# Attention products in two column ranges, maxima transposed later, scratch rows of 4 KB, normalizers loaded in another order

## The chip, the cores and the metric

The kernel runs on one core of a Trainium2 chip. A core has a matrix engine (TensorE, PE in the profile; its weight loads are shown apart as PEld), a vector engine (VectorE, DVE), an engine for functions of single elements (ScalarE, ACT), a general engine (GpSimd, POOL) and an engine that issues transfers (SyncE, SP). Each runs its own instructions in order, and they wait for one another through semaphores. SBUF is the memory that the engines work in, 128 partitions wide; TensorE writes its results to PSUM, which has eight banks of 512 float32 numbers in each partition; DRAM is reached only by DMA. The metric is the time of one execution on the device, in microseconds (us).

## The reference

One transformer block over 2048 tokens of width 640. `ln` is a layer norm without gain or bias.

```
h  = x + attention(ln(x) @ wqkv) @ wo       # 32 heads of 20; a query sees itself and the 255 keys before it
z  = gelu(ln(h) @ w_in)                     # 2048 x 1728, halves z1 and z2
g  = w_sp @ ln(z2) + b_sp                   # mixes tokens: 2048 x 2048 times 2048 x 864
h2 = h + (z1 * g) @ w_out
```

Attention is softmax(q k / sqrt(20)) v in float32, with scores outside the window set to -1e9.

## The kernel before, in words

**Stages.** To about 250 us, x is normalized, and q, k and v are computed. v stays in SBUF (`v_sb`, with a column of ones beside each head's 20 columns, so that a product with it gives the sum of the softmax's weights too). q and k are each split into three bf16 parts whose sum is the float32 number, and go to a DRAM scratch `qk_d` [2, 3, 40, 16, 1024 floats]: half of the heads, part, row of q or k, head, and 2048 bf16 tokens in 1024 floats. From about 250 to 500 us comes attention, then the projection with wo and the second layer norm, to about 570 us. The rest is the gated MLP with its large token-mixing product.

**Attention.** The 32 heads are eight groups of four. `load_stack` (L253) brings a group's q and k parts from `qk_d` into one of three slots, in twelve transfers of 20 rows, each of four heads times 4 KB; the slots hold the six pairings of parts under each other as 120 rows, so that one bf16 product gives a float32-like score. The main loop (L554) has 130 steps. Step s does, for each head `hh` of four: a product for the row maxima, 20 steps ahead (`max_item`, u1 = s + 20); the scores of 128 keys against up to 384 queries and their exponential (`score_item`, u = s); and, after the second step, for all four heads at once, the product of the exponentials with v (`pv_item`, u = s - 2). A group has 16 such steps, one for each block of 128 keys.

- `max_item` writes a bank of tag `s1`, of which there are three; VectorE adds the mask and takes the maximum to one column of `mcol` (L286). From the third block of a group on, the product is made in four strips of 32 queries and 288 keys.
- `max_rows` (L289) turns a finished group's 64 columns of maxima on TensorE (L291), splits them into three bf16 parts with four operations on VectorE, writes them to DRAM (`m_d`, L299) and reads them back as rows 120 to 122 of the slot (L301). With them the score product subtracts the maximum itself. It is called in the step in which the next group's maxima begin, four steps before its group's scores start.
- `score_item` writes one of three banks `s2` and ScalarE makes the exponential (L339); when all four heads are done, GpSimd sets to zero what lies outside the window (L341, L344). From step 109 on, two heads go together into larger tiles.
- `pv_item` adds a block's 384 query columns into banks of 512 columns (two of them, tag `pv`); where the 384 cross from one bank to the next, they are done in two ranges. After each fourth block a bank is finished, is copied by ScalarE or VectorE (`ot`, L370, L372) and goes to DRAM (`o_d`).

**The end of attention.** The sums of the softmax's weights lie in row 20 of each head in `o_d`. Once the last group has finished a bank, `inverse_sums` reads the sums of these 512 tokens for all heads, takes the reciprocal (L314) and writes it to `r_d`. `proj_early` loads and splits wo (L170 to L181), loads the outputs of 256 tokens at a time (`load_o`, L134) and their reciprocals repeated over 20 rows (its returned function, L140), multiplies (`norm_o`, L146) and splits (`split_o`, L152 to L155). Both are generators that the main loop advances by one `yield` a step.

**Order.** TensorE, VectorE and ScalarE run the attention stage in the order in which the program writes it; SP and GpSimd are ordered by a planner, as are all engines behind the stage (from L593).

Of the kernel before, what the change touches and what calls it, by code (L numbers as in the profile page):

```python
# [7 lines left out]
F32 = mybir.dt.float32  # L8
# [8 lines left out]
S = 2048  # L17
D = 640
H = 32
DH = 20  # L20
NT = S // P
# [13 lines left out]
def block_kernel(ctx, tc, x, wqk, wv, wo, w_in, wsp, bsp, w_out, out):  # L35
# [5 lines left out]
    def pool(stack, name, **kw):  # L41
        return stack.enter_context(tc.tile_pool(name=name, bufs=1, reuse_waits="tile", **kw))

    const = pool(ctx, "const")
    dram = pool(ctx, "dram", space=DRAM)

    qk_d = dram.tile([2, 3, 2 * DH, H // 2, S // 2], F32, name="qk_d")
    m_d = dram.tile([8, 3, 64, 64], F32, name="m_d")
    o_d = dram.tile([H, 32, S], F32, name="o_d")
    r_d = dram.tile([H, S], F32, name="r_d")  # L50
# [63 lines left out]
    def t1(lo, *shape):  # L114
        return view(mem["t1"], lo, *shape)

    def m1(lo, *shape):
        return view(mem["m1"], lo, *shape)
# [6 lines left out]
    def load_x2(i):  # L125
        hs[i] = mem["xh"][i % 5]
        nc.sync.dma_start(hs[i], x[i * P:(i + 1) * P, :])

    def load_o(j):

        t = slice(2 * j * P, (2 * j + 2) * P)
        ot, rs = m1(j % 2 * 2 * D, KD, 2 * P), m1(6 * D + j % 2 * 2 * P, 2 * P)
        for k in range(KD):
            nc.sync.dma_start(ot[:, k], o_d[:, 4 * k:4 * k + 4, t])  # L134
        for i in range(2):
            ots[2 * j + i] = (ot[:, :, i * P:(i + 1) * P], rs[:, i * P:(i + 1) * P])

        def load_rs():
            base = r_d[:, t]
            nc.sync.dma_start(rs, bass.AP(tensor=base.tensor, offset=base.offset, ap=[[S, H], [0, 4], [1, 2 * P]]))  # L140

        return load_rs

    def norm_o(i, eng):
        ot, rs = ots[i]
        eng.tensor_tensor(out=ot, in0=ot, in1=rs[:, None, :].to_broadcast([P, KD, P]), op=OP.mult)  # L146

    def split_o(i, eng):
        ot, _ = ots[i]
        osp = mem["osp2"] if i % 3 == 2 else t1((2 * KD + i % 3 * 2) * D, 2, KD, P)  # L150
        if eng is nc.vector:
            eng.tensor_copy(out=osp[:, 0], in_=ot)  # L152
        else:
            nc.scalar.activation(osp[:, 0], ot, AF.Copy)
        eng.tensor_tensor(out=osp[:, 1], in0=ot, in1=osp[:, 0].bitcast(F32), op=OP.subtract)  # L155
        ots[i] = osp
# [8 lines left out]
    def proj_early():  # L165
        wo_s = t1(0, 2, KD, D)
        for k in range(KD):
            if k < 4:
                raws_c[f"wo{k}"] = m1(k * D, D)
                nc.sync.dma_start(raws_c[f"wo{k}"], wo[k * P:(k + 1) * P, :])  # L170
            else:
                raws_c[f"wo{k}"] = mem["wraw"].rearrange("p a b c -> p (a b c)")[:, :D]
                nc.sync.dma_start(raws_c[f"wo{k}"], wo[k * P:(k + 1) * P, :])
        for i in range(2):
            load_x2(i)
        for _ in range(5):
            yield
        for k in range(KD):
            raw = raws_c.pop(f"wo{k}")
            nc.vector.tensor_copy(wo_s[:, 0, k], raw)  # L180
            nc.vector.tensor_tensor(out=wo_s[:, 1, k], in0=raw, in1=wo_s[:, 0, k].bitcast(F32), op=OP.subtract)  # L181
            if k in (1, 3):
                yield
        yield
        rs = [load_o(j) for j in range(2)]
        yield
        yield
        for f in rs:
            f()
        yield  # L190
        yield
        for i in range(2):
            norm_o(i, nc.vector)
            split_o(i, nc.vector)
            yield


    with ExitStack() as ab:
# [34 lines left out]
        NU = 128  # L233
# [19 lines left out]
        def load_stack(g):  # L253


            st = slot_w[g % 3]
            if g < 3:
                nc.gpsimd.memset(st[96:P, 1], ONES)
            for j, parts in enumerate(((0, 0), (0, 1), (0, 2), (1, 0), (1, 1), (2, 0))):
                for a in range(2):  # L260
                    src = qk_d[g // 4, parts[a], a * DH:(a + 1) * DH, g % 4 * 4:g % 4 * 4 + 4]
                    nc.sync.dma_start(st[j:6 * DH:6, a], src)
                    yield

# [38 lines left out]
        p_tiles, pv_tiles, inverse = {}, {}, []  # L303
# [43 lines left out]
        def pv_item(u):  # L347
            g, kb = divmod(u, NT)
            pt = p_tiles.pop(u)
            a, e = kb * P, min(S, kb * P + 384)  # L350
            while a < e:
                c = a // 512
                b = min(e, (c + 1) * 512)
                first = kb == max(0, 4 * c - 2)
                if first:
                    pv_tiles[g, c] = pv_tile(f"pv{g}_{c}")
                ps = pv_tiles[g, c]
                for hh in range(4):
                    v0 = 21 * (4 * g + hh)
                    nc.tensor.matmul(ps[32 * hh:32 * hh + 32, a - 512 * c:b - 512 * c],  # L360
                                     v_sb[:, kb, v0:v0 + 32], pt[:, hh, a - kb * P:b - kb * P],
                                     start=first, stop=(kb == 4 * c + 3), skip_group_check=True,
                                     tile_position=(0, 32 * hh))
                a = b
            if kb % 4 == 3:
                c = kb // 4
                ps = pv_tiles.pop((g, c))
                ot = tmp3.tile([P, 512], F32, tag="ot", bufs=4, name=f"ot{g}_{c}")
                if u < NU - LEAD or u >= NU - 5:
                    nc.scalar.activation(ot, ps, AF.Copy)  # L370
                else:
                    nc.vector.tensor_copy(out=ot, in_=ps)  # L372
                nc.sync.dma_start(o_d[4 * g:4 * g + 4, :, c * 512:(c + 1) * 512].rearrange("h d t -> (h d) t"), ot)
                if g == 7:
                    inverse.append(inverse_sums(c))


        if True:
# [70 lines left out]
            def split_qk(m, c, ps):  # L449
                sg = tmp.tile([P, 3, 512], BF16, tag="ta", bufs=3, name=f"sg{m}_{c}")  # L450
                rest = tmp.tile([P, 512], F32, tag="tb", bufs=2, name=f"rest{m}_{c}")
                nc.scalar.activation(sg[:, 0, :], ps, AF.Copy)  # L452
                yield
                nc.vector.tensor_tensor(out=rest, in0=ps, in1=sg[:, 0, :], op=OP.subtract)  # L454
                yield
                nc.scalar.activation(sg[:, 1, :], rest, AF.Copy)  # L456
                nc.gpsimd.tensor_tensor(out=sg[:, 2, :], in0=rest, in1=sg[:, 1, :], op=OP.subtract)  # L457
                T = S // 2
                base = qk_d[m // 5, 0, m % 5 * 8, 0, c * 256:(c + 1) * 256]
                nc.sync.dma_start(bass.AP(tensor=base.tensor, offset=base.offset,  # L460
                                          ap=[[T, P], [2 * DH * H // 2 * T, 3], [1, 256]]), sg.bitcast(F32))

# [14 lines left out]
            c = halves[0]  # L477
# [76 lines left out]
        for s in range(NU + 2):  # L554
            if s % NT == 0 and s // NT + 2 < 8:
                ld = load_stack(s // NT + 2)
            for _ in range(1 + s % 2):
                next(ld, None)
            for f in inverse:
                next(f, None)  # L560
            u1 = s + LEAD
            for hh in range(4):
                if u1 < NU:
                    max_item(u1 // NT, u1 % NT, hh)
                if s <= NU - LEAD:
                    score_item(s, hh, 1)
                elif s < NU and hh % 2 == 0:
                    score_item(s, hh, 2)
                if hh == 1 and u1 % NT == 0 and u1 <= NU:
                    max_rows(u1 // NT - 1)  # L570
                if hh == 2 + s - NU and s >= NU:
                    pre_ps.append(proj_o(s - NU, ps6[0].tile([P, 2, 512], F32, tag="sp", bufs=3,
                                                             name=f"wo_ps{s - NU}")))
                if hh == 2 and s >= 2:
                    pv_item(s - 2)
            if u1 == NU:
                psB.close()
                ps6[0] = pool(psB, "ps6t", space=PSUM)
            if s == NU - NT:
                low0.close()  # L580
                lowx.close()
                open_early(pool(early_stack, "early"))
                early = proj_early()
            if early is not None and s > NU - NT:
                next(early, None)
        for _ in early:
            pass
        for f in inverse:
# [563 lines left out]
```

## Time and profile before

| | |
|---|---|
| median of 3 runs | 1176.09 us (1174.71 to 1176.49) |
| the profiled execution | 1176.24 us, of which its span 1174.2 us |
| mean granted TensorE clock | 0.984 |
| TensorE busy | 1116.0 us, 95% |
| VectorE, ScalarE, GpSimd busy | 744.1, 543.1 and 388.8 us |
| DMA | 165.15 MB in 72122 packets, 141 GB/s in the mean |

A line of the profile names the source line (L360), the engine, the operation, what it writes and reads (out<-in), its shape and count. Behind a bar stand the busy time, the mean duration of one and the idle time of the engine just before, with what ended it. In the timeline, the first two numbers are start and duration in microseconds, and idle time before an instruction stands in square brackets with its releaser; "issue" is idle time for which the profile shows no wait. Matmuls are pipelined, so their durations overlap; the distance of their starts is what one costs. A float32 matmul appears as two, and four matmuls of 32 columns of the array, one a head, run side by side.

### The profile page before, as it was taken

To read this page: it belongs to the slowest core of one execution; us is meant where nothing else is said; L and a number is where in the kernel's file an instruction comes from. 1 tells how busy PE (TensorE), PEld (TensorE's weight loads), DVE (VectorE), ACT (ScalarE), POOL (GpSimd) and SP (SyncE) were. 2 spreads that over 40 slices of the span, in tenths; PEclk is the share of its full clock that TensorE was granted. 3 is DMA by queue.
4 is the path that set the end of the run, shared out by engine and by line. 5 is a ranking of instruction groups with operands and counts; after the bars stand their busy time and mean duration, and the time that the engine had idled before them with its cause. 6 is when DMAs were issued, how large, how long until landed. Compare 5 with 4: busy or idle time off the path is not lost. (4 is left out here: it accounts for less than half of the span.)

```text
span 1174.2 us, 25759 instructions
## 1 busy us (share of the span) xinstructions
PE 1116.0 (95%) x9888; PEld 961.9 (82%) x9888; DVE 744.1 (63%) x1949; ACT 543.1 (46%) x1125; POOL 388.8 (33%) x477
## 2 busy tenths in 40 slices
PE   6999999989999998798999999899999899999998
PEld 6998887556566565488999998899999799999998
DVE  5531125878788786479958669745548984655443
ACT  4333343248888888724346644433334431222110
POOL 4124444346555566737522046000116420000000
PEclk9999999989999999989899999999999999999999
DMA  6212453643444441659735531233341454444322
GB/s 205 66 44 87 166 194 126 260 148 111 153 161 165 154 172 52 225 174 295 261 147 191 168 103 38 66 118 116 133 139 63 130 177 150 140 132 142 90 82 81
DMA packets 72122, 165.15 MB, mean 141 GB/s; under 512 B 9128, under 2 KB 33448, under 8 KB 70056
## 3 DMA queue, kind: packets, MB, share of 16 engines
q1 hardware_dynamic: 69696, 158.27, 40.2%
q10 hardware_dynamic: 2304, 5.24, 1.1%
q8 instruction: 77, 1.26, 0.5%
q14 instruction: 45, 0.37, 0.1%
HBM read 108.83 MB, written 54.66 MB: 139 GB/s over the span
## 5 line engine op out<-in xcount | busy, mean ns | idle before, releaser
L339 ACT ACTIVATE pt<-s 128x384 f32<-128x384 f32 (+2 forms) x436 | 175.9, 488 | 27.2 <-PE s L336 18.6
L949 PE MATMUL g<-zl,aw 128*128 128x432 f32 x768 | 174.1, 362 | 7.2 <-ACT zl L617 4.9
L617 ACT ACTIVATE aw<-fx 128x512 fp32r<-128x512 f32 (+2 forms) x160 | 92.9, 595 | 185.9 <-PE g L949 123.2
L286 DVE CUSTOM_DVE_ANT_0 junk<-sm,strip 128x288 bf16<-128x288 f32 x384 | 153.4, 454 | 30.0 <-PE sm L275 27.3
L949 PEld LDWEIGHTS g<-zl,aw 128*128 128x128 f32 x768 | 144.7, 189 | 15.2 <-ACT zl L617 5.7
L949 PE MATMUL g<-ze,aw 128*128 128x432 f32 x576 | 136.7, 365 | 5.2 <-DVE row L611 3.2
L611 DVE TENSOR_TENSOR aw<-fx,aw 128x512 fp32r<-128x512 f32 (+2 forms) x152 | 108.6, 723 | 36.9 <-ACT aw L617 31.9
L949 PEld LDWEIGHTS g<-ze,aw 128*128 128x128 f32 x576 | 109.2, 192 | 12.0 <-DVE row L611 2.3
L341 POOL TENSOR_SCALAR_AFFINE_SELECT pt<-pt 128x512 f32<-128x512 f32 x128 | 82.5, 645 | 93.6 <-ACT pt L339 93.5
L360 PE MATMUL pv<-pt,v_sb 128*32 128x384 f32 (+2 forms) x1408 | 103.7, 389 | 2.6 <-POOL pt L344 2.1
L988 PE MATMUL out_ps<-wout,y_sp 128*128 128x320 f32 (+1 forms) x630 | 96.1, 309 | 0.4 <-ACT y_sp L122 0.4
L853 PE MATMUL zb<-win,aw 128*128 128x432 f32 x480 | 95.3, 359 | 0.0
L988 PEld LDWEIGHTS out_ps<-wout,y_sp 128*128 128x128 f32 (+1 forms) x630 | 94.1, 188 | 1.2 <-ACT y_sp L122 0.7
L853 PEld LDWEIGHTS zb<-win,aw 128*128 128x128 f32 x480 | 89.9, 187 | 4.7
L336 PE MATMUL s<-slot 123*32 123x288 bf16 (+5 forms) x1232 | 87.7, 288 | 3.7 <-ACT pt L339 3.2
L454 DVE TENSOR_TENSOR rest<-qk,sg 128x512 f32<-128x512 f32 x40 | 27.7, 691 | 88.9 <-ACT sg L452 88.9
L275 PE MATMUL sm<-slot 120*32 120x288 bf16 x1088 | 77.5, 294 | 1.3 <-DVE mcol L286 0.7
L336 PEld LDWEIGHTS <-slot 123*32 123x32 bf16 x1536 | 51.3, 98 | 33.2 <-issue 21.0
L457 POOL TENSOR_TENSOR sg<-rest,sg 128x512 bf16<-128x512 f32 x40 | 46.5, 1164 | 82.9 <-ACT sg L456 78.1
L344 POOL TENSOR_SCALAR_AFFINE_SELECT pt<-pt 128x512 f32<-128x512 f32 x112 | 73.7, 658 | 0.0
L611 DVE TENSOR_TENSOR row<-g,row 128x432 f32<-128x432 f32 x80 | 48.1, 604 | 37.6 <-PE g L949 32.5
L286 DVE CUSTOM_DVE_ANT_0 junk<-sm,mask 128x384 bf16<-128x384 f32 (+2 forms) x128 | 54.9, 454 | 14.1 <-PE sm L280 13.5
(177 smaller groups left out, 2186.2 us busy)
## 6 DMA issues: line engine op xcount, KB each, us to landing
slot<-qk_d SPq DMA_DIRECT2D x72, 320.0 KB
fx<-wsp_in SPq DMA_DIRECT2D x32, 512.0 KB
qk_d<-sg SPq DMA_DIRECT2D x40, 384.0 KB
fx<-hn_d SPq DMA_DIRECT2D x32, 320.0 KB
o_d<-ot SPq DMA_DIRECT2D x32, 256.0 KB
xb<-qk_d SPq DMA_DIRECT2D x24, 320.0 KB
z_d<-row SPq DMA_DIRECT2D x16, 432.0 KB
g_d<-row SPq DMA_DIRECT2D x16, 432.0 KB
```

The lines of the kernel that those rows point to most:

```text
L275: nc.tensor.matmul(ps[32 * j:32 * j + 32, :n], st[:120, 0, hh, q0:q0 + 32], st[:120, 1, hh, lo + 32 * j:lo + 32 * j + n], start=True, stop ...
L286: nc.vector.tensor_tensor_reduce(out=junk[:, :n], in0=ps[:, :n], in1=keep, scale=1.0, scalar=NEG, op0=OP.add, op1=OP.max, accum_out=m_cols ...
L336: nc.tensor.matmul(ps[32 * i:32 * i + 32, j, b:e], st[:123, 1, hh + j, k0:k0 + 32], st[:123, 0, hh + j, kb * P + b:kb * P + e], start=True ...
L339: nc.scalar.activation(pt[:, hh:hh + width, :n], ps[:, :, :n], AF.Exp, scale=SCALE)
L341: nc.gpsimd.affine_select(out=pt[:, :, :P], in_=pt[:, :, :P], pattern=[[0, 4], [1, P]], base=0, channel_multiplier=-1, compare_op=OP.is_ge ...
L344: nc.gpsimd.affine_select(out=pt[:, :, 256:], in_=pt[:, :, 256:], pattern=[[0, 4], [-1, P]], base=-1, channel_multiplier=1, compare_op=OP. ...
L360: nc.tensor.matmul(ps[32 * hh:32 * hh + 32, a - 512 * c:b - 512 * c], v_sb[:, kb, v0:v0 + 32], pt[:, hh, a - kb * P:b - kb * P], start=fir ...
L611: (eng or nc.vector).tensor_tensor(out=out, in0=a, in1=b, op=op)
L617: nc.scalar.activation(out, a, AF.Copy)
L853: nc.tensor.matmul(b[0][:, :HF], a[t][:, x, kk], win2[0][:, y, kk, h * HF:(h + 1) * HF], start=kk + x + y == 0, stop=kk == KD - 1 and x == 1)
L949: nc.tensor.matmul(ps, w[m][:, x, k], zc[k][m][:, y], start=start and k + x + y == 0, stop=stop and k == 3 and x == 1, skip_group_check=True)
L988: nc.tensor.matmul(ps[j][:, :HD], src[:w, a, k, :], e1["wout"][:w, b, k, j * HD:(j + 1) * HD], start=(k == 0 and a + b == 0), stop=(k == K ...
```

## The change

- `pv_item` becomes a generator. A step's query columns are always done in two ranges: at the bank's border as before, and otherwise 192 columns and the rest. The main loop runs the first range after head 1 and the second after head 3; before, all was done after head 2. The first product into a bank is found from whether the bank is open already.
- `max_rows` is called after head 3 in place of head 1 of the same step.
- The rows of `qk_d` are 1040 floats long in place of 1024. The four heads of a row of the slot thus lie apart in DRAM, and a stack load has 20 x 4 rows of 4 KB in place of 20 rows of 16 KB.
- `inverse_sums` advances at the end of a step in place of its start, after `proj_early`. `proj_early` starts its splits of wo a step earlier; it loads the outputs and reciprocals of the first 256 tokens ahead of those of the second 256, in place of both outputs and then both reciprocals.

```diff
-    qk_d = dram.tile([2, 3, 2 * DH, H // 2, S // 2], F32, name="qk_d")
+    qk_d = dram.tile([2, 3, 2 * DH, H // 2, S // 2 + 16], F32, name="qk_d")
...
-        for _ in range(5):
+        for _ in range(4):
             yield
...
-        rs = [load_o(j) for j in range(2)]
+        rs = load_o(0)
         yield
         yield
-        for f in rs:
-            f()
+        rs()
         yield
+        yield
+        load_o(1)()
         yield
...
-                    src = qk_d[g // 4, parts[a], a * DH:(a + 1) * DH, g % 4 * 4:g % 4 * 4 + 4]
+                    src = qk_d[g // 4, parts[a], a * DH:(a + 1) * DH, g % 4 * 4:g % 4 * 4 + 4, :S // 2]
...
-            while a < e:
+            mid = (a // 512 + 1) * 512 if a // 512 < (e - 1) // 512 else a + 192
+            for a, b in ((a, min(mid, e)), (mid, e)):
+                if a >= b:
+                    continue
                 c = a // 512
-                b = min(e, (c + 1) * 512)
-                first = kb == max(0, 4 * c - 2)
+                first = (g, c) not in pv_tiles
...
-                a = b
+                if b < e:
+                    yield
...
-                T = S // 2
+                T = S // 2 + 16
...
-            for f in inverse:
-                next(f, None)
             u1 = s + LEAD
             for hh in range(4):
...
-                if hh == 1 and u1 % NT == 0 and u1 <= NU:
+                if hh == 3 and u1 % NT == 0 and u1 <= NU:
                     max_rows(u1 // NT - 1)
...
-                if hh == 2 and s >= 2:
-                    pv_item(s - 2)
+                if s >= 2:
+                    if hh == 1:
+                        pv = pv_item(s - 2)
+                        next(pv, None)
+                    if hh == 3:
+                        next(pv, None)
...
             if early is not None and s > NU - NT:
                 next(early, None)
+            for f in inverse:
+                next(f, None)
```

## The prediction, made before the changed kernel was run

> **What bounds the kernel now.** I read the page first, then the engines' busy time by stretches, then the timeline of single steps, the waits, and the order of instructions on each queue.
>
> ```profile
> span 1174.2 us, 25759 instructions
> PE 1116.0 (95%) x9888; PEld 961.9 (82%) x9888; DVE 744.1 (63%) x1949; ACT 543.1 (46%) x1125; POOL 388.8 (33%) x477
> q8 instruction: 77, 1.26, 0.5%
> slot<-qk_d SPq DMA_DIRECT2D x72, 320.0 KB
> ```
>
> TensorE is busy almost throughout, so the whole gives no answer; the stage does. The change acts in the attention loop, about 250 to 500 us (130 steps, 16 a group), where a group takes some 30.5 us (315.62 to 346.11, by stretches shown below). One ordinary step:
>
> ```profile
> 350.08 0.83 PE L360 MATMUL pv<-pt,v_sb 128*32 128x384 f32 x8
> 350.73 0.31 PE L275 MATMUL sm<-slot 120*32 120x288 bf16 x4
> 350.98 0.31 PE L275 MATMUL sm<-slot 120*32 120x288 bf16 x4
> 351.09 0.46 DVE L286 CUSTOM_DVE_ANT_0 junk<-sm,strip 128x288 bf16<-128x288 f32 x1 [0.70 <-PE sm L275]
> 351.21 1.64 ACT L339 ACTIVATE pt<-s 128x384 f32<-128x384 f32 x4 [0.15 <-PE s L336]
> 351.47 0.45 DVE L286 CUSTOM_DVE_ANT_0 junk<-sm,strip 128x288 bf16<-128x288 f32 x1
> 351.61 0.31 PE L275 MATMUL sm<-slot 120*32 120x288 bf16 x4
> 351.77 0.24 PEld L360 LDWEIGHTS pv<-pt,v_sb 128*32 128x32 f32 x8
> 351.88 0.83 PE L360 MATMUL pv<-pt,v_sb 128*32 128x384 f32 x8
> ...
> 373.14 0.49 ACT L339 ACTIVATE pt<-s 128x384 f32<-128x384 f32 x1
> ```
>
> The columns are start, duration, engine, line; PEld is the weight load. TensorE works through head pairs (a maximum product `sm`, then a score product `s`, 0.25 us a pair: 350.73 to 350.98) and one block with v, `pv`, of 0.65 us (350.08 to 350.73). The block lets VectorE run dry (0.70 idle). The first `sm` behind it reaches VectorE 0.36 later (351.09), and its bank is free 0.52 after that (351.61): there the third next `sm` starts, since three banks rotate. Then 0.27 to the next block. 0.65 + 0.36 + 0.52 + 0.27 = 1.80, exactly the distance of the blocks (351.88 - 350.08). So no engine bounds the step; the round trip over three banks does. TensorE alone would need 4 x 0.25 + 0.65 = 1.65, ScalarE 1.53 (its spacing is (1.64 - 0.49)/3 = 0.38, the 0.49 being one exponential), VectorE 4 x 0.38 = 1.52 (351.47 - 351.09).
>
> A second loss shows in stretches with and without stack loads in flight:
>
> ```profile
> core 0: us, PE busy (x) PEld busy (x) DVE busy (x) ACT busy (x) POOL busy (x), PEclk, DMA share, GB/s
> 283.28:302.30 19.02, 16.70 (x404) 11.24 (x403) 14.83 (x77) 16.08 (x40) 10.64 (x18) 1.00 0.62 236
> 302.30:315.62 13.32, 13.15 (x276) 7.62 (x266) 11.16 (x59) 11.16 (x30) 7.75 (x13) 1.00 0.17 53
> 315.62:332.90 17.28, 16.84 (x412) 11.82 (x411) 15.19 (x79) 16.21 (x40) 10.98 (x18) 1.00 0.63 251
> 332.90:346.11 13.21, 12.82 (x265) 7.37 (x258) 10.90 (x57) 11.04 (x30) 7.39 (x13) 1.00 0.20 63
> 376.88:396.90 20.02, 17.26 (x416) 11.89 (x415) 15.56 (x80) 17.37 (x42) 11.63 (x19) 1.00 0.62 224
> 396.90:409.45 12.55, 12.45 (x257) 7.26 (x257) 10.53 (x55) 9.99 (x27) 6.75 (x11) 1.00 0.18 55
> ```
>
> With loads TensorE idles 2.32, 0.44 and 2.76 us; without, 0.17, 0.39 and 0.10. The largest piece is this, put down to no semaphore:
>
> ```profile
> 396.82 0.31 PE L275 MATMUL sm<-xb 120*32 120x288 bf16 x4 [1.57 <-issue]
> ```
>
> I take it for instructions that come late: the 77 instruction packets of 16 KB queue on the same DMA engines behind rows of 16 KB of the stack loads (320 KB over 20 partitions).
>
> **The change part by part.**
>
> *Products with v in two ranges.* The new order is pair, pair, half block, pair, pair, half block. Between an `sm` and the third next there are now three pairs and at least one half block: 0.75 + 0.32 = 1.07, more than the 0.88 (0.36 + 0.52) that the bank needs. So the wait goes and the step falls to TensorE's own 1.65. Columns are unchanged; the order of instructions has 288 more matmuls (192 + 192 where there were 384 columns), whose weight loads (eight in 0.24) fit under a half block of 0.32; only the 64-column piece, once a group, is too short, by some 0.13. What is late next is TensorE, and each fourth step ScalarE with its copy of a finished bank, so part of the 0.15 is kept there. I count 0.15 for 12 steps and 0.2 for two narrow ones: 2.2 us a group. The steps with full-width maxima (two a group) gain nothing, as TensorE already paces them. Over about 6.5 groups, until the maxima end: -14.3. Bounds: none at all, if ScalarE were the real limit, to -18. In the last 20 steps ScalarE paces (two heads an exponential), and I count nothing. The product's input is a step and a half old, so the earlier half waits for no mask on GpSimd.
>
> *The maxima transposed at the step's end.* This part costs.
>
> ```profile
> 368.99 0.30 PE L291 MATMUL mt<-ident,mcol 128*64 128x128 f32 x1
> 370.57 0.28 PE L280 MATMUL sm<-xb 120*128 120x256 bf16 x1
> 370.56 0.64 SPq L299 DMA_DIRECT2D m_d<-m  x1
> 372.68 0.25 SPq L301 DMA_DIRECT2D slot<-m_d  x1
> 376.41 0.33 PE L336 MATMUL s<-slot 123*32 123x288 bf16 x4
> 465.74 0.25 SPq L301 DMA_DIRECT2D slot<-m_d  x1
> 469.55 0.84 PE L336 MATMUL st<-slot 123*32 123x384 bf16 x12 [1.45 <-DMA slot<-m_d]
> ```
>
> From the transpose (368.99) the maxima go over VectorE to DRAM (1.57 to the issue) and back (2.12 to the second issue) before the next group's first score (376.41) may read them. Now 7.42 us lie between, and no wait shows. The old transpose stands 1.58 ahead of its step's end (370.57, the next step's first product); the new one only the second half block, 0.33. With 0.4 less in the two steps before the group the distance becomes 7.42 - 1.58 + 0.33 - 0.4 = 5.77. The chain needs at least 1.57 + 2.12 + 2.12 = 5.81, if the read lands as fast as the write did, and at most 7.42. The one group that waits shows 3.81 from issue to release (465.74 to 469.55), with other loads around it; I take 3.2 for the quiet groups, nearer to that row, as it is the same transfer: 6.87. The wait is then 1.1 us a group (0.04 to 1.65). Behind it on TensorE stand all products, so it is paid in full: six groups, +6.6 (0 to +10). For the last group the wait of 1.45 is there already and grows by what now precedes the transpose, two products and half a block: +0.8 (0 to +2, if a longer gap halves the clock for a window). On VectorE the four operations on the maxima merely change place with two maxima; on SP the two transfers keep theirs in the queue.
>
> *Rows of 4 KB.* Each of the 96 stack loads goes from 20 rows of 16 KB to 80 of 4 KB; bytes and engines stay, and nothing waits for these loads now (they have a quarter group to spare, and the DMA share is 0.6). The write of q and k keeps its 1 KB rows. What can go are the load-time idles above ordinary ones: 2.32 + 0.44 + 2.76 less 0.66 = 4.9. I take -3.5; bounds -5.5, and +1 if the added instructions bring fetches of their own.
>
> The Trainium skill (DMA: Bandwidth & Descriptors, Queues, rings and completion order) says that a DMA engine turns from one queue to the next only at packet boundaries; that agrees with idles under the loads alone, and by it 4 KB packets would take nearly all of them, 1.4 more than I count, 1164.0.
>
> *Normalizers first, and their order.* The stage's end waits on one chain:
>
> ```profile
> 496.18 0.95 DVE L314 RECIPROCAL inv<-inv 128x128 f32<-128x128 f32 x1 [5.90 <-DMA inv<-o_d]
> 498.51 1.56 DVE L146 TENSOR_TENSOR m<-m 128x640 f32<-128x640 f32 x2 [0.39 <-DMA m<-r_d]
> 500.83 1.58 DVE L155 TENSOR_TENSOR t<-m,t 128x640 fp32r<-128x640 f32 x1
> 500.95 2.42 PE L89 MATMUL wo_ps<-t 128*128 128x320 f32 x6 [5.41 <-DVE t L152]
> ```
>
> In the new order the first normalizer load stands ahead of the second chunk's inverse on SP, but on VectorE the second reciprocal (496.18) still stands ahead of the first normalization, and its input is no earlier. One cast moves ahead of two normalizations, so TensorE starts some 2 us sooner, only to wait for the low part (L155), which ends as before. I count the 0.39: -0.4 (-2 to +1). After that the planner put transposes and splits of the projection in another order:
>
> ```profile
> 540.00:550.00 10.00, 8.89 (x64) 8.65 (x63) 9.96 (x18) 3.60 (x8) 4.46 (x5) 1.00 0.96 335
> 550.00:560.00 10.00, 6.62 (x46) 6.35 (x45) 10.00 (x14) 5.12 (x10) 8.88 (x8) 0.93 0.88 254
> ```
>
> VectorE is full there (9.96 and 10.00 of 10) with the same work before and after: 0, with 3 either way.
>
> Sum: -14.3 + 6.6 + 0.8 - 3.5 - 0.4 = -10.8. The profiled execution took 1176.24 us (span 1174.2), 0.15 over the median of 1176.09, so the same to the tenth: 1176.2 - 10.8 = 1165.4.
>
> **The rivals.**
>
> *The wait for the maxima stays hidden.* If the read lands as fast as the write, 5.81 against 5.77, the 6.6 fall away: 1158.8. For it: the bound is a real row. Against: 3.81 in the group that waits. 0.17.
>
> *The idles under the loads stay.* If they aren't late instructions, or 4 KB rows hold the engines as long in sum: 1165.4 + 3.5 = 1168.9. For it: the same bytes are in flight at the same share of 0.6, and load stretch 315.62 idles only 0.44. 0.13.
>
> The Trainium skill (Runtime: NRT & Kernel Launch, Instruction fetch mechanics) gives TensorE's instruction memory 128 KiB, refilled in blocks of 16 KiB; with that much ahead a late block would starve nothing, which speaks for this rival. The trace agrees on the blocks (1.26 MB in 77) and shows no fill level.
>
> *Slower: the block was not the limit, the wait is new.* ScalarE may pace the loop: it works 16.08 to 17.37 us in the load stretches of 17.28 to 20.02. Then halves gain nothing, while the maxima come late: +6.6 + 0.8 - 3.5 - 0.4 = +3.5, 1179.7. It decides below a gain of 3.5/6.5 = 0.54 us a group. Against: ScalarE idles 0.15 a step for products, and the four terms of 1.80 close. 0.15.
>
> *The change does next to nothing*, gains and waits cancelling: 1176. 0.04.
>
> **How the numbers follow.** My forecast, with all terms near their values, has 0.46; 0.05 more goes to the projection's order, half to each side of it but still faster. Faster by over 0.2% (2.4 us, about what a measurement tells from no change): 0.46 + 0.17 + 0.13 + 0.05 = 0.81; same 0.04; slower 0.15. The range reaches down past the hidden wait with all idles gone (1157) and up to the edge of the slower case: 1156 to 1176; the slower case lies outside. The likeliest alone: 1160 to 1170.
>
> **What would show it.** Right: blocks of `pv` of about 0.32 us in pairs, ordinary steps of 1.65 to 1.7, VectorE without its 0.70; a new wait of TensorE for the maxima's transfer at each group's start, near 1.1 us; stretches with loads that idle no more than those without; 500.95 some 10 us earlier. Wrong: steps still at 1.80, ScalarE without gaps, no wait at the group's start, 1.5 us idles put down to issue, or a projection stage longer by several microseconds.

## The result, and the profile after

The changed kernel takes 1180.89 us (median of 17 runs, 1176.56 to 1190.88). The kernel before, run beside it on the same chip, takes 1172.38 (17 runs; the three shown ahead of the prediction are among them and lay at 1176). The ratio is 1.008, 95% interval 1.0061 to 1.010: **0.8% slower**, where 0.9% faster was predicted. The profiled executions differ by as much: 1184.86 us (span 1183.1) against 1176.24, both some 4 us over their medians. In the experiments below, each ratio is against the kernel before, run beside the variant, with a median of 1172.0 to 1173.5. A ratio is not the quotient of the two medians, and the two can differ by some tenths of a per cent.

The changed kernel's page, its span and its engines:

```profile
span 1183.1 us, 26900 instructions
PE 1112.6 (94%) x10464; PEld 983.4 (83%) x10464; DVE 750.2 (63%) x1949; ACT 540.1 (46%) x1125; POOL 389.6 (33%) x477
```

TensorE is busy 3.4 us less and the span is 8.9 us longer, so what came is idle time. The products with v did what was predicted of them. In the timeline of ordinary steps (start, duration, engine, line):

```profile
326.26 0.51 PE L363 MATMUL pv<-pt,v_sb 128*32 128x192 f32 x8
326.58 0.31 PE L276 MATMUL sm<-slot 120*32 120x288 bf16 x4
326.83 0.31 PE L276 MATMUL sm<-slot 120*32 120x288 bf16 x4
327.08 0.62 PE L363 MATMUL pv<-pt,v_sb 128*32 128x256 f32 x8
...
327.88 0.46 DVE L287 CUSTOM_DVE_ANT_0 junk<-sm,strip 128x288 bf16<-128x288 f32 x1
...
328.26 0.45 DVE L287 CUSTOM_DVE_ANT_0 junk<-sm,strip 128x288 bf16<-128x288 f32 x1
```

A block of 192 columns takes 0.32 us of TensorE, pairs follow at 0.25 without a break, and VectorE takes a maximum every 0.38 without the old idle of 0.70. The time went elsewhere. The waits of TensorE between 280 and 500 us (total, times, longest), first in the kernel before, then in the changed one:

```profile
PE sm L275 <- issue: 2.6, 2, 1.6
...
PE st L336 <- DMA slot<-m_d: 1.4, 1, 1.4
```

```profile
PE s L337 <- DMA slot<-m_d: 5.3, 4, 1.6
PE st L337 <- DMA slot<-m_d: 2.5, 1, 2.5
...
PE sm L276 <- issue: 2.2, 1, 2.2
PE s L337 <- DMA xb<-m_d: 2.1, 2, 1.1
```

Six groups now wait for their maxima, 5.3 + 2.1 = 7.4 us together, and the last waits 2.5 in place of 1.4. Waits put down to issue are still there. By stretches (columns as in the prediction), the first, third and fifth with stack loads in flight, the others without:

```profile
289.85:307.50 17.65, 17.07 (x492) 13.93 (x488) 16.59 (x81) 17.55 (x44) 11.39 (x19) 1.00 0.66 249
307.50:320.32 12.82, 11.34 (x261) 7.45 (x256) 10.48 (x52) 9.21 (x25) 6.98 (x12) 1.00 0.22 64
320.32:338.00 17.68, 17.23 (x496) 14.47 (x489) 16.64 (x83) 17.62 (x44) 11.54 (x19) 1.00 0.66 253
338.00:351.09 13.09, 11.13 (x257) 7.38 (x252) 10.32 (x52) 9.06 (x25) 6.83 (x12) 1.00 0.21 59
351.09:372.00 20.91, 17.44 (x446) 13.97 (x441) 15.10 (x73) 16.27 (x40) 10.00 (x17) 0.92 0.60 212
372.00:386.79 14.79, 13.03 (x307) 8.92 (x304) 12.16 (x60) 10.95 (x31) 8.37 (x14) 1.00 0.18 49
```

The stretches without loads, which idled 0.10 to 0.39 us, now idle 1.48, 1.96 and 1.76: that is for the most part the wait for the maxima. Those with loads idle 0.58, 0.45 and 3.47, where they idled 2.32, 0.44 and 2.76: the late instructions are not gone, they stand in one stretch. One chain for the maxima in the changed kernel:

```profile
342.50 0.30 PE L292 MATMUL mt<-ident,mcol 128*64 128x128 f32 x1
343.23 0.64 POOL L342 TENSOR_SCALAR_AFFINE_SELECT pt<-pt 128x512 f32<-128x512 f32 x1 [0.98 <-ACT pt L340]
343.47 0.48 DVE L298 CAST m<-mr 64x128 bf16<-64x128 f32 x1
343.82 0.64 POOL L345 TENSOR_SCALAR_AFFINE_SELECT pt<-pt 128x512 f32<-128x512 f32 x1
343.98 0.62 DVE L299 TENSOR_TENSOR m<-mr,m 64x128 bf16<-64x128 f32 x1
344.62 0.64 SPq L300 DMA_DIRECT2D m_d<-m  x1
344.99 0.27 PE L281 MATMUL sm<-slot 120*128 120x256 bf16 x1 [0.27 <-DVE mcol L287]
346.72 0.26 SPq L302 DMA_DIRECT2D slot<-m_d  x1
350.65 0.31 PE L337 MATMUL s<-slot 123*32 123x288 bf16 x4 [1.61 <-DMA slot<-m_d]
```

From the transpose to the first transfer it is 2.12 us (342.50 to 344.62), then 2.10, then 3.93 to the score's release.

### The profile page after: what moved, and what is told of

It is laid out like the page before. It is cut to its first block, busy times and chain, and to the rows that moved or that the text cites. A ratio compares the mean times of both kernels' runs of the same rounds, so it can differ in the third digit from the quotient of the medians.

```text
span 1183.1 us, 26900 instructions
## 1 busy us (share of the span) xinstructions
PE 1112.6 (94%) x10464; PEld 983.4 (83%) x10464; DVE 750.2 (63%) x1949; ACT 540.1 (46%) x1125; POOL 389.6 (33%) x477
## 5 line engine op out<-in xcount | busy, mean ns | idle before, releaser
L287 DVE CUSTOM_DVE_ANT_0 junk<-sm,strip 128x288 bf16<-128x288 f32 x384 | 156.0, 455 | 25.3 <-PE sm L276 21.6
L363 PE MATMUL pv<-pt,v_sb 128*32 128x192 f32 (+3 forms) x1984 | 130.6, 323 | 3.7 <-POOL pt L342 2.6
L337 PE MATMUL s<-slot 123*32 123x288 bf16 (+5 forms) x1232 | 92.4, 289 | 9.0 <-DMA slot<-m_d 5.3
L276 PE MATMUL sm<-slot 120*32 120x288 bf16 x1088 | 83.0, 295 | 3.2 <-issue 2.7
L363 PEld LDWEIGHTS pv<-pt,v_sb 128*32 128x32 f32 x1984 | 62.4, 111 | 14.3 <-POOL pt L342 6.5
```

The source lines that it names most:

```text
L276: nc.tensor.matmul(ps[32 * j:32 * j + 32, :n], st[:120, 0, hh, q0:q0 + 32], st[:120, 1, hh, lo + 32 * j:lo + 32 * j + n], start=True, stop ...
L287: nc.vector.tensor_tensor_reduce(out=junk[:, :n], in0=ps[:, :n], in1=keep, scale=1.0, scalar=NEG, op0=OP.add, op1=OP.max, accum_out=m_cols ...
L337: nc.tensor.matmul(ps[32 * i:32 * i + 32, j, b:e], st[:123, 1, hh + j, k0:k0 + 32], st[:123, 0, hh + j, kb * P + b:kb * P + e], start=True ...
```

## The experiments

### Each part alone

The first theories: A takes each part's worth from the two traces (steps shorter by the split, waits for the maxima, a longer stage ahead of the attention by the padding); B keeps the terms of the prediction; where a third letter stands, its sentence says what it holds. Four kernels, each with one part of the change: the split products, the late maxima (`if hh == 1` becomes `if hh == 3` at `max_rows`), the padding, the order of the normalizers. Their diffs are those of the change.

> The kernel before with the products with v in two ranges, and nothing else. Theory A, from the two traces: ordinary steps fall from 1.80 to 1.65 us as in the changed kernel, but the two steps of a group with full-width maxima grow by some 0.3 us each, so a group gains about 1 to 1.5 us and the kernel 6 to 10 us. Theory B, as forecast: 2.2 us a group, 14 us. Theory C: ScalarE paces, within 2 us of the kernel before.

> The kernel before with the transpose of the maxima after head 3 instead of head 1, and nothing else. Theory A and B: the first score of each group waits for the maxima about 1.0 us in six groups and 0.8 us more in the last: 6 to 8 us slower. Theory C: the transfer is quick enough and the wait stays hidden: no difference.

> The kernel before with the q and k scratch rows 1040 floats long, so that stack loads are 80 rows of 4 KB, and nothing else. Theory A: the stack loads hold the DMA rings longer, the stores of q and k behind them land later, and the dense stage before attention gets 4 to 7 us longer; idles under the loads in attention do not shrink: 5 to 9 us slower. Theory B, as forecast: idles shrink, 3.5 us faster.

> The kernel before with the normalizers loaded first and the inverse sums advanced at the step's end, and nothing else. Theory A and B: within 1 us of the kernel before, as the chain over the second reciprocal stays; the rival: the planner's other order of the projection makes it 2 us or more slower.

| part | median, us | ratio (95%) | predicted, us |
|---|---|---|---|
| split products | 1172.93 | 1.0001 (0.9985 to 1.0017) | -14.3 |
| late maxima | 1184.12 | 1.0091 (1.0074 to 1.0109) | +7.4 |
| padding by 16 floats | 1176.45 | 1.0031 (1.0017 to 1.0045) | -3.5 |
| normalizers | 1172.86 | 1.0004 (0.9989 to 1.0019) | -0.4 |

Two terms of B failed, one of them by the whole gain, and A misses the split as well. The late maxima cost more than the 6 to 8 us of both theories (8.7 to 12.8 by the interval), and the padding went the way of A but cost less than its 5 to 9. The split did shorten the loop. One group that nothing disturbs, in the kernel before and in the split alone, then a disturbed group of the split (stretches of exactly one group; begin, end, length):

```profile
315.62:346.11 30.49, 29.66 (x669) 19.19 (x665) 26.09 (x135) 27.25 (x69) 18.37 (x30) 1.00 0.45 170
```

```profile
314.56:343.22 28.66, 28.20 (x745) 21.97 (x741) 26.39 (x135) 26.64 (x68) 18.45 (x31) 1.00 0.51 182
343.22:376.06 32.84, 28.93 (x745) 22.03 (x741) 26.55 (x134) 26.84 (x68) 18.44 (x31) 1.00 0.42 158
```

The quiet group is 1.83 us shorter, but the next is 4.2 longer than it. In that group two waits have no releaser, this one and one of 1.75 (timeline); and between 250 and 500 us there is a wait where a group's maxima begin (waits):

```profile
353.47 0.30 PE L275 MATMUL sm<-slot 120*32 120x288 bf16 x1 [1.77 <-issue]
```

```profile
PE sm L280 <- DMA o_d<-ot: 1.4, 1, 1.4
```

These maxima don't read what the named transfer moves; they need the stack loads, and I take it for a load that landed at the same time.

### The split without stack loads

```diff
         def load_stack(g):
+            if g >= 3:
+                return
```

> The products with v in two ranges alone, with the stack loads of the groups 3 to 7 left out (these groups work on stale stacks, so the output is not the reference's; the amount of work on every engine stays). Alone, with the loads, the split shortened a group's steps where nothing disturbs them by 1.63 us (28.66 against 30.3), some 9 us over the stage, and gained nothing in time (ratio 1.0001). Theory 1: the gain is given back under the stack loads, where TensorE's instructions come late. Then, without the loads, this kernel is 7 to 10 us faster than the kernel before with the same loads left out (e6), and some 11 to 14 us faster than the kernel before, about 1160. Theory 2: the gain is given back elsewhere, behind the attention stage or before it. Then this kernel equals e6 within 2 us, and its attention steps are still shorter. Theory 3: the quiet steps aren't shorter over the whole stage: equal, with equal steps.

> The kernel before with the stack loads of the groups 3 to 7 left out (stale stacks, the output is not the reference's). The control of e5. The prediction read 4.9 us of idle time of TensorE under three loads as instructions that come late. Theory 1 (late instructions under the loads): 4 to 6 us faster than the kernel before, about 1167, and no idle time of 1.5 us put down to issue between 283 and 400 us. Against it: the idles belong to the order of work, and the time stays within 2 us of 1172.3.

Measured: the split without loads 1162.58 us, ratio 0.9893 (0.9874 to 0.9912); the kernel before without loads 1170.0, ratio 0.9962 (0.9945 to 0.9979). The split is then worth 0.9893 / 0.9962 = 0.9931, or -8.1 us. One group with the split:

```profile
312.17:340.85 28.68, 28.23 (x745) 21.83 (x741) 26.40 (x135) 26.66 (x68) 18.38 (x31) 1.00 0.13 44
```

All groups from the second to the sixth with the split now take 28.7 us, and those of the control 30.1 to 30.8. Theory 1's first half holds: the loads take the gain back. The loads cost the kernel before 0.4% and the split 1.1%.

Are the instructions late? A stretch of some 17.8 us at the start of a group, with the instruction packets in it (queue, packets, MB, share), first in the split with loads, then without:

```profile
343.22:361.00 17.78, 13.94 (x383) 11.04 (x379) 13.09 (x66) 13.85 (x34) 10.19 (x17) 1.00 0.64 247
```

```profile
q8 instruction: 2, 0.03, 0.7%
```

```profile
340.85:358.60 17.75, 17.35 (x496) 14.31 (x489) 16.92 (x86) 17.69 (x45) 11.99 (x21) 1.00 0.10 34
```

```profile
q8 instruction: 4, 0.07, 1.7%
```

TensorE took 383 + 379 = 762 instructions on two packets, against 985 on four: one packet for 381 against one for 246. Under the loads the packets come late, and TensorE stands in "issue". The trace of the split alone shows it stall by stall. Between its two stalls, which end at 353.47 and 360.21, TensorE takes just one packet's worth, 128 matmuls and 128 weight loads (19776 of them came in 77 packets in the kernel before, 257 a packet):

```profile
353.46:360.20 6.74, 4.99 (x128) 3.97 (x128) 4.65 (x22) 4.92 (x12) 3.68 (x6) 1.00 0.67 274
```

Narrow windows of the DMA view place the packets at 350.9 and 357.8, so each stall ends 2.5 us behind a packet. It is the same in the kernel before: packets at 292.0 and 394.3, stalls that end at 294.51 and 396.82.

### Smaller packets: the padding without its offset

```diff
-    qk_d = dram.tile([2, 3, 2 * DH, H // 2, S // 2], F32, name="qk_d")
+    qk_d = dram.tile([2, 3, 2 * DH, H // 2, S // 2 + 128], F32, name="qk_d")
```

> The kernel before with only the scratch rows padded, by 128 floats in place of 16: the rows are 4 KB packets again, but begin at multiples of 512 bytes as they did before. With 16 floats (64 bytes) of padding the kernel took 3.6 us more (ratio 1.0031). If the packets' number and size cost that: the same, 1.002 to 1.0045. If the rows' place in DRAM costs it: within 0.1% of the kernel before.

> The products with v in two ranges, and the scratch rows padded by 128 floats (4 KB packets at multiples of 512 bytes); loads unpaced, maxima and normalizers as in the kernel before. The padding by 16 floats, which is in the change, took 0.3% alone, the padding by 128 nothing. If 4 KB packets let TensorE's instruction packets through sooner, as the prediction had it (-3.5), it shows best here, where the split makes the stalls under the loads largest (they hold some 7 us): 1166 to 1170, ratio 0.994 to 0.997. If a backlog of the same bytes delays an instruction packet by the same time whatever the size of its packets: as the split alone, 1.000.

Measured: 1173.57 us, ratio 0.9998 (0.9982 to 1.0014), for the padding by 128 floats alone; 1172.05, 1.0007 (0.9985 to 1.0029), with the split. So packets of 4 KB as such cost nothing and gain nothing, and the 0.3% of the padding by 16 floats goes with where its rows lie, not with the packets' size. Late instructions are not cured. In the same group of the split with 4 KB packets:

```profile
343.60:361.00 17.40, 14.05 (x385) 11.37 (x381) 13.20 (x66) 13.86 (x35) 10.16 (x17) 1.00 0.64 233
```

```profile
q8 instruction: 2, 0.03, 0.7%
```

Again two packets for 766 instructions, and 3.35 us of idle time; the stalls end 2.4 and 2.5 us behind a packet, as with 16 KB. What 4 KB rows do change lies ahead of the attention. There the store of q and k queues behind the stack loads, and ScalarE waits for it to land before it may reuse the buffer. From 90 to 256 us these waits of ScalarE (L452, for the DMA qk_d<-sg) take 9.0 us in the kernel before, and 17.2 and 18.5 with 16 and 128 floats of padding. They double with either padding. Since only one of the two is slower, these waits don't carry the 0.3%; where that lies stays open, and the profiled executions can't show it, as both took the same time (1174.92 and 1174.83 us).

### The loads paced

```diff
-                    nc.sync.dma_start(st[j:6 * DH:6, a], src)
+                    d = nc.sync.dma_start(st[j:6 * DH:6, a], src)
+                    if last_exp:
+                        tc.add_manual_dep(d.ins, last_exp[0], after_exp)
...
-            for _ in range(1 + s % 2):
+            for _ in range(1 + (s % NT in (0, 6))):
                 next(ld, None)
```

SP runs ahead of the loop; in the split alone a group's twelve loads go out in 11 us (timeline of SP):

```profile
313.90 5.20 SPq L262 DMA_DIRECT2D slot<-qk_d  x7
...
319.70 5.06 SPq L262 DMA_DIRECT2D slot<-qk_d  x5
```

Here each load waits for the last exponential of the step before.

> The products with v in two ranges alone, with the stack loads paced: each load also waits for the last exponential of the step before the one in which the program writes it, one load a step and two in the steps 0 and 6 of a group, so 12 loads go out over ten steps instead of within some 10 us. All work and all bytes stay. Theory 1 (TensorE's instruction packets come late behind a backlog of load packets): no backlog builds up, the packets start every 256 instructions again, the stalls of 1 to 2 us that the split alone shows under the loads go, and the time falls most of the way to the split without loads (1162.6): 1163 to 1168, ratio 0.991 to 0.996. Theory 2 (any load traffic beside the attention costs TensorE the same, however it is spread): as the split alone, ratio 1.000. Theory 3 (the last loads now land too late for the next group's maxima): slower, with a wait for a load at the group's step 12.

> The kernel before with the same pacing of the stack loads and nothing else. Theory 1: its stalls under the loads go too, which leaving the loads out showed to be worth 0.4% (ratio 0.9962): ratio 0.996 to 0.999. Theory 2: 1.000.

Measured: 1187.33 us, ratio 1.0112 (1.0081 to 1.0142), with the split; 1183.36, 1.0079 (1.0052 to 1.0106), without. Theory 3 decides the time. With the split, a stretch with its instruction packets, and later in the same group a wait:

```profile
321.00:339.00 18.00, 17.55 (x500) 14.60 (x496) 17.20 (x87) 17.95 (x45) 12.25 (x21) 1.00 0.65 217
```

```profile
q8 instruction: 4, 0.07, 1.6%
```

```profile
343.85 0.23 PE L283 MATMUL sm<-slot 120*128 120x128 bf16 x1 [2.65 <-DMA slot<-qk_d]
```

At the same traffic (DMA share 0.65), 18 us of load hold four instruction packets for 996 instructions, and TensorE idles 0.45. As long as the paced loads keep up, the packets are on time, so it isn't load traffic as such that makes them late. Three other groups look the same over the 16 us in which their loads are issued (0.32 to 0.40 idle). But the stalls are not gone. From 250 to 500 us four waits put down to issue are left, 5.3 us in all against 4.2 in the split alone. They end at 311.30, 376.90, 407.52 and 439.91, at the next group's first maxima or up to 2.5 us ahead of them, where loads that were issued earlier have yet to land: a backlog has built up there after all. And the twelve loads, 3.9 MB, which need some 17 us at the 236 GB/s of a load stretch, now land in this group 2.65 us after the next group's first maxima want them. The granted clock then falls too:

```profile
341.00:351.00 10.00, 7.35 (x89) 2.97 (x85) 4.21 (x24) 4.74 (x11) 3.04 (x6) 0.74 0.18 53
```

The control met neither of its expectations. Its waits put down to issue fell from 2.6 us to 0.5, but its loads land late too: the first maxima of two groups wait 2.02 and 1.92 us for them (309.15, 438.15).

One more run joined the split, these paced loads and rows padded by 128 floats. If small packets helped, it was to be 1 to 4 us faster than the split with paced loads, and the same within 0.1% if the pacing had already removed the backlog. It took 1184.94 us, ratio 1.0138 (1.0091 to 1.0185): by the intervals not to be told from 1.0112, and no sign of a gain. Here three waits for late loads take 7.0 us.

Pacing over eight steps in place of ten (two loads in each even step, one in each odd) was to have both:

> As the split with paced loads, but 12 loads in eight steps in place of ten (two in each even step, one in each odd). Paced over ten steps, the stalls in the middle of the groups went, but the last load landed some 2 us after the next group's first maxima needed it. Issued two steps (3.3 us) earlier, the last load lands in time if the transfers keep up (12 loads take some 17 us on their engines). Theory 1 then: stalls mostly gone and no late load, 1164 to 1169, ratio 0.992 to 0.997. If the backlog is there again, because 12 loads in 13 us are more than the engines move: as the split alone, 1.000, with stalls behind the step 5.

> The kernel before with the loads paced over eight steps. Control of the split with the same pacing: by theory 1 between 0.996 and 0.999; with the backlog as before 1.000; with late loads over 1.002.

Measured: 1176.09 us, 1.0037 (1.0018 to 1.0056), with the split; 1174.87, 1.0020 (1.0005 to 1.0035), without. Neither expectation: some stalls of both kinds are left. With the split, TensorE's waits from 250 to 500 us begin so:

```profile
PE pv L366 <- issue: 3.8, 3, 2.3
...
PE sm L283 <- DMA o_d<-ot: 1.8, 2, 1.5
```

The last row stands again where a group's maxima begin. At neither pace did the loads both leave the instructions alone and land in time.

### Fewer, larger loads

The stack's rows were ordered by pairing, so that pairings which read the same or neighbouring parts go in one transfer: 60, 60, 40, 40, 20 and 20 rows.

```diff
-            for j, parts in enumerate(((0, 0), (0, 1), (0, 2), (1, 0), (1, 1), (2, 0))):
+            for j, n, p, dp in ((0, 3, (0, 0), (0, 1)), (3, 2, (1, 0), (0, 1)), (5, 1, (2, 0), (0, 0))):
...
+                                  ap=[[dp[a] * part, n], [H // 2 * (S // 2), DH], [1, 4 * (S // 2)]])
```

> The products with v in two ranges, with a group's stack loaded in six transfers of 60, 60, 40, 40, 20 and 20 rows in place of twelve of 20 (the rows of the stack are ordered by pairing, so that pairings that read the same or neighbouring parts lie together; bytes and row size stay). With 20 rows the DMA share in the load stretches is 0.62 to 0.67 of 16 engines, near 10 of 16. Theory 1 (the ten engines are the bottleneck: their backlog of some 17 us delays instruction packets and lets the last load land as the next group needs it): if 60 and 40 rows go over more engines, the share rises towards 0.9 and the loads end some 4 to 6 us earlier; the wait at a group's step 12 goes, and the split keeps a part of its gain: 1164 to 1170, ratio 0.992 to 0.998. Against it: if the memory and not the engines sets the rate, or the rows stay on ten engines, the loads take as long as before, ratio 1.000.

> The kernel before with the same six transfers. Control: its groups are 1.6 us longer and none of its steps waits for a landing, so only its stalls by late instructions (some 3 us by the runs without loads) can change: ratio 0.997 to 1.000 by theory 1, 1.000 if the rate does not rise.

Measured: 1473.29 us, ratio 1.2557 (1.2533 to 1.2581), and 1466.01, 1.2499 (1.2475 to 1.2522). The rows went over fewer engines, not more. In the split's second group, with the loads in flight throughout:

```profile
390.50:409.20 18.70, 18.22 (x520) 14.99 (x513) 17.69 (x88) 18.64 (x47) 12.63 (x21) 1.00 0.37 117
409.20:447.00 37.80, 1.53 (x44) 1.06 (x36) 1.67 (x8) 1.89 (x5) 2.45 (x4) 0.58 0.16 67
```

The share of 0.16 is some three of 16 engines, and the transfer's source has 3 (or 2) parts as its outermost dimension. The Trainium skill (DMA: Bandwidth & Descriptors, Why a DMA increments its semaphore by 16 and not by 1) says that a transfer goes over the largest number of engines up to 16 that divides the slowest dimension of both its sides; the trace agrees, with 0.16 here and 0.62 to 0.67, near 10 of 16, for 20 rows. So this run doesn't test the spread that it was meant to. It does show loads in flight on a few engines that delay no instruction: until the missing load is needed, 18.7 us hold 0.48 of idle time and four instruction packets for 1033 instructions.

### The change with one part undone

> The changed kernel with the scratch rows at 4 KB distance again, so 16 KB packets in the stack loads: split, late maxima and normalizers stay. If the padding costs the 3.6 us inside the whole change that it cost alone (1.0031), this comes to about 1177, ratio 1.0045, and the stage before the attention is some 4 to 6 us shorter than in the changed kernel. If the smaller packets help the changed kernel against late instructions, as the prediction had it (-3.5), this is slower than the changed kernel, 1184 and more. If the sum of the parts held, it would be 0 + 10.7 + 0.5, ratio 1.0095.

> The changed kernel with the maxima transposed after head 1 again; split, padding by 16 floats and the order of the normalizers stay. If the late maxima cost the 0.9% inside the whole change that they cost alone (1.0091), this comes to about 1172, ratio 0.999; by the sum of the parts alone (0 + 3.6 + 0.5) 1.0035. The step before a group's first score falls from 2.6 to 3.2 us back to 1.45.

Measured: without the padding 1180.17 us, ratio 1.0057 (1.0030 to 1.0084); without the late maxima 1171.35, 0.9982 (0.9964 to 1.0000). The late maxima cost 1.0% inside the change, all of its loss and a little more; the padding 0.2%, which is within the intervals. Both ratios are lower than the product of their parts, 1.0096 and 1.0036, and so is that of the whole change (1.008 against 1.0127). So the parts don't add: the split seems to gain 0.4 to 0.5% beside others, though the first of these differences is no larger than its intervals. One would expect that the late maxima make a group longer again and the split's late loads come in time. In the changed kernel no group's first maxima wait for a load, but without the padding one still does (1.29 us at 306.70), so the traces don't bear this out, and the cause stays open. The variant without the late maxima is the fastest complete one, and can't be told from the kernel before.

## Why the prediction was wrong, point by point

**Split products, -14.3: right loop, wrong sum.** The working of the 1.80 holds: ordinary steps fell to 1.65 and VectorE's idle went. Two things were mis-sized. The group gained 1.8 us (30.49 to 28.66), not 2.2, as the steps in which a bank is copied gained nothing and the full-width ones lost. And the sentence on the loads, that nothing waits for them since they have a quarter group to spare, was true of the old length only. A group's loads need some 17 us on their engines however long the group is, and the split moves the need for them forward; it also takes 745 matmuls in 28.7 us where there were 669 in 30.5, from the same delayed packets. Without loads the split gives -8.1 (some 3 us either way, by the intervals of the two ratios); with them nothing. The prediction treated loads and split as two separate terms, and they were one.

**Maxima transposed late, +7.4: the wait right, a cost put at nothing.** Alone, this part costs 10.7 us (8.7 to 12.8). In that run six groups wait 4.5 + 2.3 = 6.8 us for their maxima (6.6 predicted), and the last waits 2.2 in place of 1.4 (0.8 predicted); the sum behind the 6.6 has a slip without weight, as 1.57 + 2.12 + 3.2 is 6.89 and not 6.87. What failed is the sentence that VectorE's four operations merely change place. The chain to the first transfer took 2.12, not 1.57, because the last two operations now coincide with GpSimd's selects: 0.48 and 0.62 us (343.47, 343.98), where they had taken 0.26 and 0.28. They also hold up the next maxima, so that TensorE waits for a bank (344.99). With the late maxima alone, a group's two full-width steps take 5.18 us between first exponentials (373.94 to 379.12), 4.83 in the kernel before (368.31 to 373.14); six times 0.35 is 2.1. 6.8 + 0.8 + 2.1 = 9.7, within the interval.

**Rows of 4 KB, -3.5: no such gain.** The cause was named rightly, instructions that come late behind the loads, and its whole worth in the kernel before was right too (0.38% by the run without loads, some 4.5 us). The remedy was wrong. The rule by which the prediction let small packets through was that of the Trainium skill (DMA: Bandwidth & Descriptors, Queues, rings and completion order): an engine turns from queue to queue at packet boundaries. The prediction drew from it that 4 KB packets bring the instructions in time; that did not come out, as two came in 17.4 us among small data packets, no more than among large ones. A backlog delayed them at either size that was tried. The rival that the idles stay was right on this term, though not by the rule that stood beside it. That rule, of an instruction memory that holds eight blocks (the Trainium skill, Runtime: NRT & Kernel Launch, Instruction fetch mechanics), would hide a block that comes some 130 instructions late; the trace does not agree, as TensorE takes 256 instructions between two stalls and starves again.

**Normalizers first, -0.4: nothing measurable** (1.0004). As predicted, TensorE began the projection after a shorter wait (3.10 us in place of 5.41) and then waited for the low part (L155):

```profile
508.02 1.06 PE L89 MATMUL wo_ps<-t 128*128 128x320 f32 x4 [3.10 <-DVE t L152]
...
510.98 1.44 PE L89 MATMUL wo_ps<-t 128*128 128x320 f32 x4 [1.90 <-DVE t L155]
```

3.10 + 1.90 = 5.00 is 0.4 less than 5.41, the term as forecast, but too small to be told from nothing in the time; with the reordering alone TensorE waits 5.16 in one piece. The start that was to come some 10 us earlier than 500.95 came 7 us later, at 508.02, as the loop gained nothing.

**The rivals.** The slower one gave 1179.7, near the result, for another reason: it had ScalarE pacing the loop, so that the halves gain nothing. They do gain; the loads take it back. No rival had loads that come late for a shorter group.

## What to carry to other kernels

Before a gain per step is multiplied by the number of steps, ask which transfers run at a fixed rate beside those steps: how long they occupy their DMA engines, when the last must have landed, and what they do to the instruction packets; a slack of only a quarter of a group, and waits put down to issue, were the signs here. A few operations moved to another place in a step cost what they cost there, so look at what runs beside them on other engines. And change the size or spread of a transfer only with the number of engines that it will use in mind.

## What the runs showed of the hardware that was not expected

- **VectorE stretched by GpSimd.** The two operations in the kernel before, then in the changed one (count, shortest/median/longest in ns):

```profile
L297 DVE CAST m<-mr x8: 220/261/549, 236.6 to 462.8; 64x128 bf16<-64x128 f32 x8
L298 DVE TENSOR_TENSOR m<-mr,m x8: 282/283/285, 236.8 to 463.3; 64x128 bf16<-64x128 f32 x8
```

```profile
L298 DVE CAST m<-mr x8: 220/476/480, 243.5 to 472.3; 64x128 bf16<-64x128 f32 x8
L299 DVE TENSOR_TENSOR m<-mr,m x8: 284/616/619, 243.8 to 472.5; 64x128 bf16<-64x128 f32 x8
```

  The cast and the subtraction on 64x128 take nearly twice as long and more beside a select, and each ended just behind the select's end (343.95 against 343.87, 344.60 against 344.46). In the last group the cast began at 472.28, 0.02 ahead of a select: it kept its 0.22, and that select took 0.70 in place of 0.64. The Trainium skill (SBUF — State Buffer, Who interferes with whom) says that VectorE's casts, in modes that use two ports, and its operations with two inputs in SBUF contend with GpSimd for shared ports, and that whoever comes second waits. The trace agrees on who is held up. It does not show a wait for the whole of the other's operation, as the two ended 0.08 and 0.14 behind the selects, less than the 0.26 and 0.28 that they take alone.
- **Instruction packets late behind a backlog of data, in large packets or small:** 381 TensorE instructions a packet under a backlog of 16 KB packets, 383 (766 in two packets) under one of 4 KB packets, 249 at the same traffic where paced loads kept up. TensorE ran again 2.4 to 2.6 us behind a packet.
- **A transfer of 60 rows in three parts ran at some three engines' rate** (share 0.16, 67 GB/s), one of 20 rows at ten's.
- **The place of rows in DRAM:** 64 bytes of padding a row cost 0.3%, 512 bytes nothing, with the same packets. The cause is not seen.
